# Three added waits in a transformer block whose instruction order is written out by hand

## The chip, the core and the metric

The kernel runs on one NeuronCore of one Trainium2 chip. Five engines work from instruction streams of their own: PE (matrix multiply; PEld is its weight load), DVE (vector), ACT (scalar functions), POOL (general, also elementwise) and SP, which here only issues DMAs. They meet through semaphores alone. The metric is the device time of one execution in microseconds (us); lower is better. Three runs of the kernel before took 273.07, 271.93 and 273.23 us, the median is 273.07.

## The reference

One block of a network on a sequence of 2048 tokens of 448 channels: a modulated layer norm, attention in a sliding window of 256 keys with 16 heads of 28 channels, a gated residual, a second modulated layer norm, a gated MLP whose gate mixes along the sequence with a 2048 x 2048 matrix, and a second gated residual.

```python
mod = silu(c) @ w_mod                      # sa, ca, ga, sb, cb, gb: six rows of 448
h = layernorm(x) * (1 + ca) + sa
q, k, v = split(h @ wqkv)                  # 16 heads of 28
p = softmax(where(0 <= i - j < 256, q @ k.T * 28 ** -0.5, -1e9))
x = x + ga * ((p @ v) @ wo)
h = layernorm(x) * (1 + cb) + sb
z = gelu(h @ w_in)                         # 2 * 896 columns
g = w_sp @ layernorm(z[:, 896:]) + b_sp[:, None]
out = x + gb * ((z[:, :896] * g) @ w_out)
```

## The kernel before

The tokens are 16 tiles of 128, taken in four blocks of four tiles. A tile of `x` is normalised with tokens on partitions (`xn`), turned so that channels lie on partitions (`hT`), modulated, and multiplied by the padded weights of q and k (`WQK`) and of v (`wv`). For the first two blocks PE does the turning (lines 679 and 701), for the later two and for the attention output a DMA transpose does. Scores are exponentiated by ACT into `PA`, masked by DVE, and multiplied by v on PE. After that come the output product with `wo_g` (line 1007), the second norm, the MLP's input products, the mixing along the sequence with `wspA` and `wspB` (line 1133), and the output product (line 1152).

Nothing is scheduled while the kernel runs. Python code first makes a list of operations, each numbered in the order in which it was added, each with a list of the operations that it depends on. The table `ORDER` then says, word by word, which operation goes next on which engine (`p` is PE, `a` ACT, `v` DVE, `g` POOL, `s` SP), and which buffer it takes. `Sched.order` walks the table. `Sched.waits` finds for each operation the semaphore waits that its dependences need, leaving out those that an earlier wait on the same engine already covers, and `emit` writes them ahead of its instruction. A wait holds everything that stands behind it on its engine, since each engine works in order.

The operations that this document follows are these.

- `pad` (lines 590 to 595) copies one 128-row slice of the q or the k weights from `wq_st` into the padded layout of `WQK`, 32 columns a head. There are four slices of each. The last two of k, operations 138 and 139, are copied by POOL at line 595, one behind the other. Then POOL builds the attention mask.
- `stats` and `norm` (lines 597 to 632): DVE takes mean and variance of a tile, POOL raises the variance to the power -1/2 (line 611), DVE forms mean times that (line 615), and DVE or ACT or POOL writes the normalised tile. Operation 163 is the normalised fourth tile of the first block, on DVE at line 623. PE's second set of eight turns (line 679) waits for it.
- The first block's products with `WQK` are at line 726, with the slices of the weights taken one after the other.
- In the third block the four channel slices of `hT` are modulated in place, two by POOL, one by ACT (line 669), one by DVE (line 671, operation 292). PE's line 764 needs all four.
- The gate is folded into `wo`: four POOL products (lines 586 and 587), which stand in the order 129, 130, 128, 131 behind POOL's two slices of `hT`.
- `load2` (lines 400 to 406) splits a load in two, since 448 rows are three times 128 and 64. Operation 20 is the second piece of the load of `w_o`, 64 rows, issued by SP at line 405. On SP it stands between DMA transposes of `w_sp` (line 481).
- Operation 376 is the first group of score matmuls with 64 queries, 64 instructions at line 876.

```python
t_wog = [pool(1.05, lambda e, kc=kc: e.tensor_tensor(wo_g[:, kc, :], wo_g[:, kc, :], gg_sb[:, 0, :], ALU.mult),
              [t_wo, t_gg[0]], -13.0 + 0.1 * kc) for kc in range(DC)]
```

Of the kernel before, what the change touches and what calls it, by code (L numbers as in the profile page):

```python
# [19 lines left out]
2.a 30.v 40.g 41.g 42.g 0.s 31.v 32.v 33.v 43.g 44.g 3.a 4.s 38.g 34.v 5.s 35.v 36.v 37.v 45.g 6.s 59.p.0 60.p.0 52.p.0 54.a 53.a 7.s 51.a 61.p.1 46.g  # L20
146.v 8.s 62.p.1 63.p.0 147.v 1.s 140.v 64.p.0 148.g 9.s 141.v 149.g 65.p.0 142.v 10.s 66.p.0 143.g 150.v 151.a.0 67.p.0 68.p.0 69.p.0 70.p.0 11.s
39.g 144.v 56.p.0 145.v.1 134.g 14.s 57.p 58.p 12.s 167.p.1 132.a 114.v 164.p.2 113.v 133.v 135.g 73.p.3 168.v 16.s 74.p.0 165.v 75.p.0 169.a 152.v
13.s 176.p.0.3 166.a 177.p.4.5 15.s 153.v 158.v 154.g 178.p 179.p 137.a 155.g 17.s 180.p 159.v 181.p 160.v 136.v 185.p 161.g 156.v 183.p 182.p 189.a
190.p.1.2 187.v 191.p.6.7 138.g 157.a.0 162.v 192.p 193.p 163.v.1 139.g 170.p.3 173.p.5 171.v 194.p 234.v 172.v 230.v 228.v 235.v 55.v 231.v 232.v
229.v 233.v 195.p 184.p 198.p 196.p 197.p 174.a 175.a 199.p 186.a 204.p.3 200.a 208.a 203.a 206.p.0 205.p.5 207.p.3 220.p.1 209.v 188.v 211.v 202.a
201.a 210.a 376.p.0.0 377.a.0 378.a 222.p.0 226.p.6 368.p.0.1 221.v 47.g 48.g 236.g 49.g 50.g 237.g 238.v 240.v.0 239.v.1 241.g.2 223.v 242.v.3 227.v
212.p.0 216.v 246.p.1 243.p.4 247.v 244.v 248.v 369.a.0 370.a 372.p.0.2 373.a 374.a 213.p.0 275.v 217.v 245.v 371.v 273.v 277.v 375.v 274.v 115.p.1
380.p.0.1 381.a.1 116.a 382.a 29.s 840.s 20.s 841.s 18.s 846.s 214.p.0 249.p.3 251.p.4 218.a 250.a 384.p.0.3 215.p.7 253.p.0 255.p.3 385.a 252.a 386.a
388.v 279.v 278.v 379.v 280.v 276.v 219.v 397.p.0.1 263.p.4 271.p.1 281.g 282.g 383.v 256.v 283.v 254.v 326.v 324.v 264.v 272.v 398.a.0 399.a
389.p.0.2 224.p.0 257.p.2 285.g.0 284.g.1 286.g.2 287.g.3 390.a.2 391.a 393.p.0.0 394.a 259.p.1 260.a 395.a 225.v 387.v 258.v 400.v 392.v 261.p.0  # L30
401.p.0.1 262.v 552.p.0 535.p.3 536.p 537.p 538.p 569.p.2 570.p 553.p 554.p 539.v 396.v 402.a.3 403.a 405.p.0.4 571.p 555.p 269.p.2 572.p 540.v.0
409.v 556.v 406.a 270.a 407.a 418.p.0.3 419.a.0 404.v 557.v.1 267.p.2 26.s 118.s 21.s 842.s 117.s 19.s 119.s 289.s 288.s 120.s 291.s 290.s 121.s 124.s
123.s 558.s 586.p.0 265.p.0 408.v 268.v 322.v 266.v 410.p.0.1 587.p 588.p 589.p 295.a 293.g 294.g 292.v 300.p.0 573.v 323.v 574.v.2 590.v 320.v 301.v
411.a.0 420.a 414.p.0.0 412.a 296.p.1 302.p.0 415.a 416.a 129.g 130.g 128.g 131.g 325.v 591.v.1 297.v 327.v 321.v 303.v 421.v 413.v 328.g 329.g 417.v
422.p.0.1 423.a.1 575.s 125.s 541.s 845.s 592.s 298.p.1 306.p.0 426.p.0.0 299.a 424.a 427.a 304.p.1 603.p.0 604.p 605.p 606.p 431.p.0.1 307.a 428.a
542.p.0 310.p.4 432.a.2 433.a 430.v 425.v 330.v 607.v 305.v 608.v.0 543.v 311.v 544.v 331.g.0 332.g.1 333.g.2 334.g.3 439.p.0.2 440.a.0 441.a 620.p.3
308.p.0 621.p 435.p.0.0 436.a 437.a 429.v 545.v 309.v 434.v 622.p 593.p.0 623.p 443.p.0.1 444.a.3 445.a 312.p.3 314.p.4 442.v 624.v 594.v 625.v.1
595.v 438.v 315.v 843.s 336.s 338.s 337.s 609.s 335.s 626.s 447.p.0.3 448.a 313.a 449.a 637.p.4 638.p 559.p.2 639.p 460.p.0.0 461.a.1 462.a 451.v
560.v 446.v 610.p.3 654.p.1 640.p 596.v 450.v 611.v 641.v 341.g 597.g 612.v 642.v.2 561.v 452.p.0.3 655.p 656.p 657.p 576.p.3 339.g 658.v 577.v 562.v
659.v.1 546.g 340.g 342.g 598.g 599.g 453.a.0 454.a 456.p.0.0 318.p.0 627.p.1 457.a 458.a 464.p.0.1 465.a.1 455.v 613.v 563.g 547.g 548.g 628.v 564.g  # L40
565.g 463.v 600.g.0 349.p.3 343.p.1 468.p.0.0 350.a 469.a 466.a 470.a 566.g.1 319.v 578.v 344.v 459.v 671.p.4 672.p 347.p.3 348.v 472.v 481.p.0.3
345.p.2 316.p.4 673.p 674.p 482.a.0 346.a 483.a 473.p.0.1 474.a.2 475.a 351.p.3 467.v 317.v 471.v 688.p.3 689.p 23.s 839.s 25.s 27.s 122.s 643.s 24.s
629.v 675.v 352.v 676.v.0 601.g 614.g 549.g.2 567.g 550.g 660.s 602.s 477.p.0.0 690.p 691.p 355.p.0 478.a 479.a 485.p.0.1 486.a.3 487.a 644.p.3
353.p.4 476.v 579.v 484.v 580.g 581.g 356.v 480.v 645.v 489.p.0.4 490.a 491.a 705.p.0 706.p 707.p 708.p 582.g 583.g.0 615.g 584.g 692.v 630.v 354.v
693.v.1 493.v 494.p.0.0 495.a.0 496.a 363.p.1 661.p.0 502.p.0.1 492.v 709.v 631.g 632.g 616.g 488.v 710.v.2 662.v 633.g 497.v 28.s 551.s 126.s 127.g
844.s 677.s 364.v 722.p.0 723.p 678.p.4 679.v 503.a.0 504.a 498.p.0.4 724.p 725.p 359.p.1 499.a 500.a 506.p.0.0 507.a.1 505.v 726.v 727.v.0 634.g.2
360.v 501.v 663.v 514.v 635.g 585.s 694.s 568.s 22.s 728.s 711.s 357.p.2 361.p.0 358.a 510.p.0.2 511.a 739.p.3 740.p 741.p 742.p 508.a 523.p.0.1
695.p.4 646.v 743.v 744.v.1 729.p.1 362.v 696.v 664.v 647.v 648.v 730.v 524.a.0 512.a 515.p.0.4 365.p.4 712.p.1 516.a.2 815.g 617.g.0 816.g 814.g
649.g 650.g 513.v 509.v 618.v 680.v 713.v 366.a 519.p.0.2 517.a 520.a 525.a 756.p.2 757.p 758.p 759.p 527.p.0.3 521.a 528.a.3 531.a 529.a 532.a 745.s
636.s 619.s 746.p.0 651.g.1 652.g 518.v 817.g 863.p.2 864.p.0 865.p 866.p 681.v 760.v 761.v.0 526.v 530.v 665.g 666.g 667.g 682.g 683.g 534.v 522.v  # L50
668.v.0 533.v 669.g 790.p.2 791.p 773.p.3 792.p 793.p 774.p 775.p 776.p 731.v 747.v 794.v 762.s 367.s 653.s 875.a 867.a 763.p.0 670.s 684.g 685.g.2
686.g 795.v.0 697.v 732.v 698.v 733.v 777.v 699.g 700.g 714.v 813.g 778.v.1 764.v 701.v 715.v 734.g 735.g 702.v.1 748.v 703.v 736.v.0 881.p.1 882.p.0
883.p 884.p 1003.p.2 1004.p.3 1005.p 1006.p 819.a 821.a 820.a 885.a 892.a 737.g 818.g 687.s 796.s 779.s 1008.a 1009.a 1007.a 898.p.1 899.p.0 900.p
901.p 1010.a 910.a 902.a 780.p.0 797.p.1 916.p.0 917.p.1 918.p 919.p 704.s 869.v 765.v 766.v 767.v 876.v 886.v 716.g 717.g 718.g 719.v.2 738.s 720.v
810.g 768.g 887.v 769.v 749.v 750.v 893.v 894.a.0 770.v.1 751.g 752.g 771.v 888.v 753.g.0 781.v 889.v 782.v 721.s 783.v 825.v 822.g 824.a 830.s 772.s
855.s 798.v 784.v 920.a 785.g 823.v 799.v 754.v 755.s 800.v 786.v 787.v.2 788.v 927.a 928.v 801.g 802.g 803.g 804.v.1 877.a.0 951.p.2 952.p.0 805.v
929.a.1 933.p.3 953.p 954.p 955.a 962.a 934.p.1 935.p 936.p 937.a 1035.p.2 1036.p.0 1037.p 1038.p 911.g 912.a.0 945.a 789.s 806.s 853.s 859.s 834.s
833.s 849.s 838.s 851.s 852.s 832.s 831.s 856.s 835.s 836.s 837.s 857.s 858.s 861.s 860.s 850.s 848.s 854.s 847.s 862.s 957.v 878.v 868.v 870.v 956.v
938.v 903.v 904.v 890.g 946.g 828.v 826.a 1027.p.1 1041.a 1042.a 1040.a 1039.a 947.a.0 827.v 829.v 921.v 963.v 922.v 939.v 905.v 906.g 968.p.3 969.p.0
970.p 971.p 972.a 980.a 923.v 895.v 958.v 907.g 959.g 913.g 891.v 924.v 930.v 871.v 872.g 873.g 874.g 973.v 974.v 940.v 908.g 981.g 960.g 961.v 896.g  # L60
964.a.0 986.p.2 987.p.3 988.p 990.a 909.g 811.g 992.v 991.v 993.v 994.v 941.v 995.g 996.v 914.g 942.g 1043.p.0 989.p 997.a 965.g 943.g 944.g 1028.p.2
1029.p 1030.p 1044.p.3 1045.p 1032.a 1031.a 1034.a 948.v 975.v 976.g 998.v 1033.a 1011.p.1 1046.p 999.a.0 982.a.1 983.g 931.g 1050.a 1049.a 1047.a
1048.a 1012.p.2 1013.p 1014.p 1015.a 1016.a 1018.a 1017.a 1019.p.3 1051.p.0 1052.p.1 1053.p 1054.p 1020.p.2 1021.p 1022.p 1055.a 1056.a 1058.a 1025.a
1024.a 1057.a 1023.a 1026.a 1000.v 915.v 984.g 977.g 949.g 925.g 879.g 978.v 897.v 985.v 966.g 926.v 950.v 1001.g 932.v 880.v 1002.v 979.g 967.v
1062.p.0 1063.v.0 1065.p.1 1066.v.1 1067.g 1068.p.0 1104.p.1 1105.v.1 1064.g 1106.g 1161.p.2 1173.p.1 1170.p.3 1176.p.4 1174.v.0 1162.v.1 807.g 1175.g
# [1171 lines left out]
```

## Time and profile before

| | us |
|---|---|
| median of three runs (lowest, highest) | 273.07 (271.93, 273.23) |
| the profiled execution | 273.21 |
| its span, first to last instruction | 271.5 |
| PE busy in the span | 262.0 (96%) |
| DVE busy | 160.2 (59%) |
| ACT busy | 132.2 (49%) |
| POOL busy | 124.9 (46%) |

PE is busy nearly throughout, and DVE and ACT are nearly full in the first 110 us, where attention runs; after that PE is alone. The share of an average says little about a single wait. What the change touches lies in the first 48 us, and is read from the timelines of the engines and from the chain of work that ended last, which goes back from the last instruction to what released it at each step. The granted clock of PE is full throughout.

### The profile page before, as it was taken

The numbers are of one execution on the slowest core, as the hardware profiler recorded it, in microseconds if no ns is written. First come the engines' busy times: TensorE is split into PE (matmuls) and PEld (weight loads), VectorE is DVE, ScalarE is ACT, GpSimd is POOL, SyncE is SP. The second block draws the span as 40 slices with busy tenths as digits, with TensorE's granted clock in tenths as the row PEclk, the third lists the DMA queues.
The fourth block names the chain that finished last, engine by engine and source line by source line (L and its number), as shares of the span: only waits on it lengthen the run. The fifth ranks groups of instructions, "written<-read, shape, count | busy, mean of one in ns | idle before, by whom it ended". The sixth has DMA issues, their size and how long they took to land.

```text
span 271.5 us, 6856 instructions
## 1 busy us (share of the span) xinstructions
PE 262.0 (96%) x2918; PEld 135.5 (50%) x2918; DVE 160.2 (59%) x357; ACT 132.2 (49%) x189; POOL 124.9 (46%) x184
## 2 busy tenths in 40 slices
PE   7898999999999999999999999999999999999995
PEld 3654455556476656444444444444444444444453
DVE  6898999999999999885746111123212102251233
ACT  3598999999999994799988300000000000000000
POOL 8530619325949668762499033445313100464130
PEclk9999999999999999999999999999999999999999
DMA  7998532857943567875999970000000000100203
GB/s 224 304 277 171 141 84 46 111 86 117 187 95 80 87 70 161 99 157 106 167 181 195 173 151 0 0 4 0 17 0 2 0 0 0 53 17 0 68 19 101
DMA packets 66777, 25.46 MB, mean 94 GB/s; under 512 B 57845, under 2 KB 66042, under 8 KB 66746
## 3 DMA queue, kind: packets, MB, share of 16 engines
q1 hardware_dynamic: 66472, 24.56, 47.1%
q8 instruction: 23, 0.38, 0.6%
q10 hardware_dynamic: 274, 0.46, 0.5%
q14 instruction: 8, 0.07, 0.1%
HBM read 9.53 MB, written 1.84 MB: 42 GB/s over the span
## 4 chain that ended last, share of the span: by engine, by line
PE 65%; DVE 21%; POOL 5%; ACT 5%; DMA 2%; issue 1%; DVEq 0%; POOLq 0%
PE ps L1133 36%; PE ps L1152 8%; PE ps L1109 7%; PE ps L1063 6%; DVE PA L919 4%; DVE PA L955 3%; DVE st_all L603 3%; PE ps L764 2%; ACT PA L909 2%; POOL rs_all L611 2%; DMA hT<-xn 2%; DVE Vaug L806 2%; PE ps L876 1%; PE ps L1007 1%; DVE o_sb L999 1%
## 5 line engine op out<-in xcount | busy, mean ns | idle before, releaser
L1140 POOL TENSOR_TENSOR z1T<-tmpg,z1T 128x512 bf16<-128x512 bf16 x28 | 31.8, 1154 | 76.2 <-DVE tmpg L1137 76.2
L909 ACT ACTIVATE PA<-ps 128x1536 bf16<-128x1536 f32 (+4 forms) x64 | 60.4, 974 | 2.7 <-PE ps L876 1.7
L1137 DVE TENSOR_TENSOR tmpg<-ps,bsp_bc 128x512 bf16<-128x512 f32 x28 | 19.0, 689 | 62.4 <-PE ps L1133 58.2
L1133 PE MATMUL ps<-wspB,z 128*128 128x512 bf16 x224 | 49.3, 379 | 0.0
L1133 PE MATMUL ps<-wspA,z 128*128 128x512 bf16 x224 | 49.2, 379 | 0.0
L1133 PEld LDWEIGHTS ps<-wspA,z 128*128 128x128 bf16 x224 | 21.8, 98 | 26.5 <-issue 0.4
L1133 PEld LDWEIGHTS ps<-wspB,z 128*128 128x128 bf16 x224 | 21.9, 98 | 26.3
L1163 DVE TENSOR_TENSOR fin<-ps,x_sb 128x448 bf16<-128x448 f32 (+2 forms) x18 | 10.0, 569 | 28.7 <-PE ps L1152 28.7
L611 POOL TENSOR_TENSOR rs_all<-ve_all,neghalf 128x1 f32<-128x1 f32 (+1 forms) x31 | 22.6, 732 | 5.2 <-DVE ve_all L608 3.3
L984 PEld LDWEIGHTS ps<-Vaug,PA 128*128 128x128 bf16 x720 | 20.4, 96 | 5.3 <-issue 1.3
L984 PE MATMUL ps<-Vaug,PA 128*128 128x32 bf16 x720 | 22.2, 176 | 0.4 <-DVE x_sb L1012 0.2
L1063 PE MATMUL ps<-w_in,hT 64*128 64x448 bf16 x224 | 22.3, 349 | 0.2 <-ACT z L1074 0.2
L1152 PE MATMUL ps<-w_out_g,z1T 128*128 128x448 bf16 (+2 forms) x126 | 22.2, 332 | 0.0
L1109 PE MATMUL ps<-hT,w_in 64*128 64x512 bf16 x196 | 21.8, 376 | 0.0
L919 DVE TENSOR_TENSOR PA<-PA,mask 128x1024 bf16<-128x1024 bf16 (+1 forms) x32 | 21.7, 683 | 0.0
L764 PE MATMUL ps<-hT,WQK 128*128 128x512 bf16 x80 | 19.6, 380 | 0.5 <-DVE hT L671 0.5
L603 DVE BATCH_NORM_STATS2 st_all<-x_sb 128x6 f32<-128x448 bf16 x32 | 19.3, 611 | 0.0
L876 PE MATMUL ps<-qT,KT 32*64 32x64 bf16 (+3 forms) x768 | 17.9, 223 | 0.9 <-ACT PA L909 0.3
L608 POOL TENSOR_SCALAR ve_all<-mv_all 128x1 f32<-128x1 f32 (+1 forms) x19 | 6.5, 344 | 25.2 <-DVE mv_all L606 21.0
L940 ACT ACTIVATE PA<-ps 128x1536 bf16<-128x1536 f32 (+1 forms) x16 | 16.4, 1027 | 1.7 <-PE ps L876 1.5
L955 DVE TENSOR_TENSOR PA<-PA,mask 128x2048 bf16<-128x2048 bf16 x14 | 17.0, 1215 | 0.0
L1152 PEld LDWEIGHTS ps<-w_out_g,z1T 128*128 128x128 bf16 x126 | 11.7, 98 | 10.1 <-POOL z1T L1140 0.2
(115 smaller groups left out, 334.7 us busy)
## 6 DMA issues: line engine op xcount, KB each, us to landing
w_in<-in_B_w_in_dram SPq DMA_DIRECT2D x8, 224.0 KB, 4.1
out_dram<-fin SPq DMA_DIRECT2D x15, 112.0 KB, 1.7
x_sb<-in_A_x_dram SPq DMA_DIRECT2D x3, 448.0 KB, 5.3
wmod<-in_w_mod_dram SPq DMA_DIRECT2D x1, 1344.0 KB, 9.7
w_out_g<-in_B_w_out_dram SPq DMA_DIRECT2D x1, 784.0 KB, 5.1
bsp_bc<-in_B_b_sp_dram SPq DMA_DIRECT2D x1, 512.0 KB, 4.3
x_sb<-in_A_x_dram SPq DMA_DIRECT2D x2, 224.0 KB, 3.4
wmod<-in_w_mod_dram SPq DMA_DIRECT2D x2, 224.0 KB, 5.3
```

The costliest lines, as they stand in the source:

```text
L603: st = [dve(0.62 if True else 0, lambda e, t=t, ci=ci, s=s: e.bn_stats(st_all[:, slot, t, ci, :], s()), deps(t), prio) for ci, s in enumer ...
L611: rs = pool(0.41 + 0.155 * len(tiles), lambda e: e.tensor_tensor(rs_all[:, slot, a:b], ve_all[:, slot, a:b], neghalf[:, 0:b - a], ALU.pow) ...
L764: m = pe(4 * MMS, [lambda e, h=h, g=g, kc=kc, tb=tb: e.matmul(ps[:, h.slot[0], :], lhsT=WQK[:, kc, 4 * g:4 * g + 4, :].rearrange("p a b -> ...
L909: return e.activation(cols(place(kb, hf) + 64 + 768 * a, [[384, 2 * (b - a)], [1, w]]), ps[:, h.slot[0]:h.slot[0] + b - a, 2 * n * w:(2 * ...
L919: main_mk[(kb, hf)] = dve(0.15 + 512 * tri / 1920.0, lambda e, hf=hf, tri=tri: e.tensor_tensor(cols(place(kb, hf) + 64, [[384, 8], [192, t ...
L955: return e.tensor_tensor(cols(a, [[d, 2], [384, 16], [1, 64]]), cols(src(), [[0, 2], [64, 16], [1, 64]]), mask_ap([[64 if m else 192, 2], ...
L984: fns.append(lambda e, hO=hO, hd=hd, bi=bi, kb=kb, nb=nb, j=j, c=(2 * t + k) * 384 + 128 * (j - kb), half=half: e.matmul(ps[:, hO.slot[0], ...
L1063: return lambda e, kc, p0, start, stop: e.matmul(ps[:, hs[t % 2].slot[hf], 0:D], lhsT=hT[p0:p0 + 64, kc, t * 128:(t + 1) * 128], rhs=w_in[ ...
L1109: return lambda e, kc, p0, start, stop: e.matmul(ps[:, hs[b // 2].slot[b % 2], :], lhsT=w_in[p0:p0 + 64, kc, ft * 128:(ft + 1) * 128], rhs ...
L1133: m = pe(16 * MMS, [lambda e, h=h, si=si, ft=ft, tb=tb: e.matmul(ps[:, h.slot[0], :], lhsT=z2[:, si, ft * 128:(ft + 1) * 128], rhs=(wspA i ...
L1140: u = pool(1.16, lambda e, ht=ht, ft=ft, tb=tb: e.tensor_tensor(z1T[tb][:, ft, :], tmpg[:, ht.slot[0], :], z1T[tb][:, ft, :], ALU.mult), [ ...
L1152: return [lambda e, ft=ft: e.matmul(ps[:, h.slot[0], c0:c1], lhsT=z1T[t // 4][:, ft, (t % 4) * 128:(t % 4 + 1) * 128], rhs=w_out_g[:, ft, ...
```

## The change

The table `ORDER` is written as one line, and its words are interleaved in another way. The order within each engine, and the buffer of every operation, are the same as before. What differs is a second table, `AFTER`. Each of its pairs adds the first operation to the dependences of the second.

```diff
 ORDER = """
-2.a 30.v 40.g 41.g 42.g 0.s 31.v 32.v 33.v 43.g 44.g 3.a 4.s 38.g 34.v 5.s 35.v 36.v 37.v 45.g 6.s 59.p.0 60.p.0 52.p.0 54.a 53.a 7.s 51.a 61.p.1 46.g
...
 """
+
+AFTER = "376-20 163-138 292-130"
...
         self.prog = {e: [] for e in ENGS}
+        for pair in AFTER.split():
+            first, then = pair.split("-")
+            self.ops[int(then)].deps.add(self.ops[int(first)])
         for word in ORDER.split():
```

Line numbers of the changed kernel are lower by 48 from the loop over `ORDER` on. Its waits differ from those before in three places. The words in brackets name the semaphores that a row waits for: an engine's own, or that of a load.

The first place is POOL at about 10 us: the last two copies of k's weights, with the normalisation of tile three ahead of them and the building of the mask behind. Before:

```order
L608 TENSOR_SCALAR ve_all<-mv_all 128x1 [waits dve]
L611 TENSOR_TENSOR rs_all<-ve_all,neghalf 128x1 [waits pool]
L611 TENSOR_TENSOR rs_all<-ve_all,neghalf 128x1 [waits dve]
L595 COPY WQK<-wq_st 128x16x28 [waits d_wkb]
L595 COPY WQK<-wq_st 128x16x28 [waits d_wkc]
L510 MEMSET mask_60 128x320
```

And changed:

```order
L560 TENSOR_SCALAR ve_all<-mv_all 128x1 [waits dve]
L563 TENSOR_TENSOR rs_all<-ve_all,neghalf 128x1 [waits pool]
L563 TENSOR_TENSOR rs_all<-ve_all,neghalf 128x1 [waits dve]
L547 COPY WQK<-wq_st 128x16x28 [waits d_wkb,dve]
L547 COPY WQK<-wq_st 128x16x28 [waits d_wkc]
L462 MEMSET mask_60 128x320
```

The first of the two copies now waits for DVE as well, for operation 163, the normalised fourth tile; the second copy and the mask stand behind it.

The second place is POOL at about 43 us, where the four products that fold the gate into `w_o` stand behind two slices of `hT`. Before:

```order
L671 TENSOR_SCALAR hT<-hT,modT 128x512 [waits d_h1T2]
L671 TENSOR_SCALAR hT<-hT,modT 128x512
L587 TENSOR_TENSOR wo_g<-wo_g,gg_sb 128x448 [waits d_wob,d_woc,d_woa,d_gg0]
L587 TENSOR_TENSOR wo_g<-wo_g,gg_sb 128x448 x3
L608 TENSOR_SCALAR ve_all<-mv_all 128x4 [waits dve]
```

And changed:

```order
L623 TENSOR_SCALAR hT<-hT,modT 128x512 [waits d_h1T2]
L623 TENSOR_SCALAR hT<-hT,modT 128x512
L539 TENSOR_TENSOR wo_g<-wo_g,gg_sb 128x448 [waits d_wob,d_woc,d_woa,d_gg0]
L539 TENSOR_TENSOR wo_g<-wo_g,gg_sb 128x448 [waits dve]
L539 TENSOR_TENSOR wo_g<-wo_g,gg_sb 128x448 x2
L560 TENSOR_SCALAR ve_all<-mv_all 128x4 [waits dve]
```

The first product is issued as before; the second waits for DVE's slice of `hT` (operation 292), and the last two follow it.

The third place is SP at about 16 us, with two more transposes, a load of `x` and a load of `w_in` queued behind the second piece of `w_o`. Before:

```order
L481 DMA_TRANSPOSE wspA<-in_B_w_sp_dram 128x1024
L405 DMA wo_g<-in_A_wo_dram 64x448
L481 DMA_TRANSPOSE wspA<-in_B_w_sp_dram 128x1024
L409 DMA x_sb<-in_A_x_dram 128x4x448
L481 DMA_TRANSPOSE wspA<-in_B_w_sp_dram 128x1024
L445 DMA w_in<-in_B_w_in_dram 128x896
L577 DMA mod_rows<-gg_sb 1x448 [waits act]
```

And changed:

```order
L433 DMA_TRANSPOSE wspA<-in_B_w_sp_dram 128x1024
L357 DMA wo_g<-in_A_wo_dram 64x448 [waits pe]
L433 DMA_TRANSPOSE wspA<-in_B_w_sp_dram 128x1024
L361 DMA x_sb<-in_A_x_dram 128x4x448
L433 DMA_TRANSPOSE wspA<-in_B_w_sp_dram 128x1024
L397 DMA w_in<-in_B_w_in_dram 128x896
L529 DMA mod_rows<-gg_sb 1x448 [waits act]
```

The load now waits for PE, for operation 376, the first group of 64-query scores, and everything behind it on SP waits with it.

More of the change, by code (lines that the diff above doesn't have):

```diff
@@ L24 @@
[L24 to L63, printed above, removed]
@@ L64 @@
-1024.a 1057.a 1023.a 1026.a 1000.v 915.v 984.g 977.g 949.g 925.g 879.g 978.v 897.v 985.v 966.g 926.v 950.v 1001.g 932.v 880.v 1002.v 979.g 967.v
-1062.p.0 1063.v.0 1065.p.1 1066.v.1 1067.g 1068.p.0 1104.p.1 1105.v.1 1064.g 1106.g 1161.p.2 1173.p.1 1170.p.3 1176.p.4 1174.v.0 1162.v.1 807.g 1175.g
-1163.g 812.g 1177.v.0 1178.g 1069.v.1 1070.g 809.g 1158.p.1 1171.v.0 1164.p.0 1165.v.1 1166.g 1172.g 1167.p.2 1074.p.0 808.g 1159.v.1 1160.g 1168.v.0
-1169.g 1179.p.1 1180.p 1181.v.0 1183.p.2 1187.p.1 1075.v.0 1076.g 1184.p 1188.p 1189.v.1 1098.p.0 1077.p.1 1099.v.0 1100.g 1059.p.0 1060.v.0 1078.v.1
@@ L68 @@
-1079.g 1061.g 1071.p.3 1072.v.1 1185.v.2 1073.g 1092.p.0 1083.p.1 1080.p.2 1089.p.3 1143.p.4 1086.p.5 1110.p.6 1131.p.7 1087.v.3 1182.s 1132.v.0
-1081.v.0 1111.v.1 1112.g 1133.g 1125.p.5 1101.p.2 1126.v.1 1102.v.0 1103.g 1107.p.5 1127.g 1093.v.0 1082.s 1190.s 1088.s 1094.g 1095.p.0 1137.p.2
-1090.v.0 1144.v.1 1145.g 1084.v.1 1108.v.1 1096.v.0 1097.g 1109.g 1116.p.0 1117.v.3 1138.v.0 1139.g 1128.p.1 1113.p.0 1134.p.2 1085.s 1114.v.1 1115.s
-1129.v.0 1186.s 1118.s 1135.v.1 1136.g 1130.g 1091.s 1140.p.0 1141.v.0 1142.g 1119.p.1 1122.p.0 1149.p.2 1155.p.3 1152.p.4 1146.p.5 1191.p.6 1123.v.0
```

6 lines of the change are left out of this document (1 added, 5 removed).

## The prediction

> **What bounds the kernel now.** I read the page first, then the chain that ended last, then the timelines of the engines around the three places.
>
> ```profile
> span 271.5 us, 6856 instructions
> PE 262.0 (96%) x2918; PEld 135.5 (50%) x2918; DVE 160.2 (59%) x357; ACT 132.2 (49%) x189; POOL 124.9 (46%) x184
> q8 instruction: 23, 0.38, 0.6%
> ```
>
> PE is nearly full, so only time in which PE stands idle can be won. The chain (start, length, what), cut to the stretches that the change touches:
>
> ```profile
> 11.46 0.90 DVE xn L623
> 12.40 0.41 PE ps L679 x4
> ...
> 17.19 0.79 PE ps L876 x64
> ...
> 20.54 0.84 PE ps L701 x15
> 21.38 1.09 issue
> 22.47 0.24 PE ps L701
> 22.74 1.00 DVE hT L715 x2
> ...
> 44.08 1.13 DVE hT L671
> ```
>
> The operations that the added waits favour, DVE's L623 and L671, both lie on the chain, and between them is a hole of 1.09 us in which PE waits for nothing that the profile shows. From 45 us on the chain passes between engines that wait for each other, and no load from memory stands in it, so I take what is won at 45 us to reach the end.
>
> **The copies of w_k.** POOL, DVE and PE around 11 us, with uncontended repeats of the two DVE forms at 10.33 and 19.65:
>
> ```profile
> 10.86 1.06 POOL L595 COPY WQK<-wq_st 128x448 bf16<-128x448 bf16 x2
> 16.25 0.23 POOL L608 TENSOR_SCALAR ve_all<-mv_all 128x4 f32<-128x4 f32 x1 [3.67 <-DVE mv_all L606]
> ...
> 7.84 0.73 DVE L688 TENSOR_SCALAR hT<-ps,modT 128x256 bf16<-128x256 bf16 x2
> 10.33 0.15 DVE L615 SCALAR_TENSOR_TENSOR ve_all<-mv_all,rs_all 128x1 f32<-128x1 f32 x1
> 11.00 0.42 DVE L615 SCALAR_TENSOR_TENSOR ve_all<-mv_all,rs_all 128x1 f32<-128x1 f32 x1
> 11.46 0.89 DVE L623 TENSOR_SCALAR xn<-x_sb,mv_all,rs_all 128x448 bf16<-128x448 bf16 x1
> 19.65 0.38 DVE L623 TENSOR_SCALAR xn<-x_sb,mv_all,rs_all 128x448 bf16<-128x448 bf16 x1
> ...
> 12.40 0.62 PE L679 MATMUL ps<-ident,xn 128*128 128x128 bf16 x8 [0.80 <-DVE xn L623]
> 14.28 1.92 PE L726 MATMUL ps<-hT,WQK 128*128 128x256 bf16 x16 [0.27 <-ACT hT L686]
> ```
>
> While POOL copies (10.86 to 11.92), L615 takes 0.42 for 0.15 us and L623 takes 0.89 for 0.38; L623 ends where the copies end plus its own 0.38. With the copies behind it DVE gains 0.27 + 0.51 = 0.78, and L623 ends at 11.57 in place of 12.35. PE was idle for 0.80 before its turns, so these start at about 11.63, 0.77 earlier.
>
> The copies then run from about 11.63 to 12.69, 0.77 later. PE's turns end near 12.1 and its next products want the first copy, ready at 12.2: about 0.1 us, which the 0.27 idle before 14.28 takes up. The mask behind them on POOL is covered by the 3.67 us for which POOL then waits. DVE's next operation beside the copies is L688, whose two at 7.84 took 0.73 together although POOL copied then too, so I charge it nothing. Thus PE comes 0.77 us earlier to L701, whose first fifteen end at 20.6 in place of 21.4.
>
> Whether that is worth anything the hole decides, and this is the term I choose rather than read:
>
> ```profile
> 22.47 0.23 PE L701 MATMUL ps<-ident,xn 128*128 128x128 bf16 x1 [1.09 <-issue]
> ...
> 22.74 1.00 DVE L715 TENSOR_SCALAR hT<-ps,modT 128x512 bf16<-128x512 bf16 x2 [1.17 <-PE ps L701]
> ...
> 10.58 5.57 SPq L481 DMA_TRANSPOSE wspA<-in_B_w_sp_dram  x1
> ...
> q1 hardware_dynamic: 1973, 2.16, 112.1%
> ...
> q8 instruction: 1, 0.02, 33.6%
> q14 instruction: 1, 0.01, 10.4%
> ```
>
> Queue q8 moved 0.38 MB in 23 pieces, some 16 KB each, and PE's 5836 instructions over 23 are about 254 a piece, so I read q8 as PE's instructions. The q1 row is the queues' answer for 12.0 to 19.8 us: the load queue alone, no instructions. The q8 and q14 rows are that for 19.8 to 20.0: one piece on each instruction queue, within 0.2 us of each other, after nothing for 7.8 us. Two streams released together point at the rings, which were working off what SP had issued (the transpose at 10.58 held SP for 5.57 us), not at PE's own pace. None of that moves. So I take the piece to arrive at the same time, PE to resume at 22.47, and the hole to grow from 1.09 to about 1.86. This edit is then worth 0. Its bounds are 0 and 1.86: the hole could move along (0.77 won) or close (0.77 + 1.09). Below 0 it falls only if instructions come later than now, which the fourth rival prices. I take 0 because of the two rows on q8 and q14.
>
> [...]
>
> **The products of w_o.**
>
> ```profile
> 43.00 4.09 POOL L587 TENSOR_TENSOR wo_g<-wo_g,gg_sb 128x448 bf16<-128x448 bf16 x4
> 48.70 0.23 POOL L608 TENSOR_SCALAR ve_all<-mv_all 128x4 f32<-128x4 f32 x1 [1.60 <-DVE mv_all L606]
> ...
> 43.99 1.20 DVE L671 TENSOR_SCALAR hT<-hT,modT 128x512 bf16<-128x512 bf16 x1
> 119.78 0.40 DVE L1032 TENSOR_SCALAR hT<-hT,modT 128x512 bf16<-128x512 bf16 x1
> ...
> 45.25 1.04 PE L764 MATMUL ps<-hT,WQK 128*128 128x512 bf16 x4 [0.51 <-DVE hT L671]
> 53.37 0.93 PE L1007 MATMUL ps<-wo_g,hT 128*128 128x448 bf16 x4
> ```
>
> Four products in 4.09 us are 1.02 each. The first ends at about 44.02, just after L671 is issued; the second then runs beside L671, which takes 1.20 us, while the same form at 119.78, without POOL, takes 0.40. Held back, the second leaves L671 to end at about 44.4 in place of 45.2: 0.80 won on DVE. PE has other work until 45.25 - 0.51 = 44.74, so PE wins 0.51; the rest is lost. The three held products start at about 44.5 and end at 47.6, 0.5 later: POOL then waits 1.60 us anyway, and PE first reads `wo_g` at 53.37. The half microsecond of POOL work that is new to the time after 47.1 falls on DVE work that I charge nothing, since the copy-like DVE operations at 45 to 47 ran beside these same products before.
>
> **The load.** The group it waits for ends at 17.98, so it goes out at 18.0 in place of 16.20, at most 1.8 us later.
>
> ```profile
> 16.20 0.57 SPq L405 DMA_DIRECT2D wo_g<-in_A_wo_dram  x1
> 16.82 2.63 SPq L481 DMA_TRANSPOSE wspA<-in_B_w_sp_dram  x1
> 19.50 0.58 SPq L409 DMA_DIRECT2D x_sb<-in_A_x_dram  x1
> ...
> SPq L577 <- ACT gg_sb L571: 4.0, 1, 4.0
> ```
>
> Behind it SP issues two transposes, a load of x and one of w_in, and then waits 4.0 us for ACT: 1.8 fits in. The piece itself is wanted at 43.00. The load of x would leave at 21.3 (19.50 + 1.8) at the latest; with its form's 5.3 us to landing it is there near 26.6, and DVE takes its first statistics at 31.85:
>
> ```profile
> 31.85 1.14 DVE L603 BATCH_NORM_STATS2 st_all<-x_sb 128x6 f32<-128x448 bf16 x2
> ...
> x_sb<-in_A_x_dram SPq DMA_DIRECT2D x3, 448.0 KB, 5.3
> ```
>
> Worth 0 directly; what the later transposes do to the instruction queue is the last rival.
>
> **The sum.** 0 + 0.51 + 0 off the profiled execution's 273.21 gives 272.7. The median is 0.14 below that execution, which puts the forecast at 272.5 for a median, 0.2% faster. I call within 0.5% (1.4 us) the same, since that is about what a measurement of this kernel tells from no change: its own three runs lie 0.5% apart.
>
> **The rivals.**
> First, the hole is PE's own and moves along: 0.77 + 0.51 = 1.28, so 271.8 as a median. For it: the profile names no fetch. Against: the two instruction queues' common arrival. 0.14.
> Second, the hole closes, because PE asks for its block 0.77 us earlier and that puts it ahead of the transposes in the rings: 0.77 + 1.09 + 0.51 = 2.37, so 270.7. For it: DVE's idle 1.17 before 22.74 leaves room. [...] 0.14.
> Third, the wait at 43 us does nothing, since L671 meets the first product in its place. They overlap by 0.03 us; if POOL came 0.5 us later against DVE it would be so. Then 273.1. 0.10.
> Fourth, slower: the postponed transposes now stand ahead of PE's next block. In 22.4 to 30.3 us PE runs 251 instructions, so the block after is wanted near 30.3; its piece is in the queues' answer for 24.4 to 24.8.
>
> ```profile
> 22.40:30.30 7.90, 7.61 (x125) 3.70 (x126) 7.56 (x19) 7.19 (x10) 0.81 (x2) 1.00 0.66 178
> ...
> q8 instruction: 1, 0.02, 20.3%
> ```
>
> The first piece came at 19.9 and PE went on at 22.47, 2.6 later; by that the next is there at 27.2, 3.1 before it is wanted. A lateness of 1.8 is hidden; beyond 3.1 each us costs one, and above about 5 us the 0.51 is eaten and 0.5% lost. Two holes like the present one more would give 273.1 - 0.5 + 2.2 = 274.8. 0.09.
>
> **The numbers.** The forecast itself has 0.53. Faster by over 0.5% means below 271.7: all of the second rival, and not quite half of the first, which ends at that bound, 0.20. Slower: the fourth and a remainder, 0.10. The same: 0.70. The range takes in the forecast, the first and the third rival and reaches toward the second: 270.9 to 273.7.
>
> **What would show it.** L623 of the first block near 0.38 us and L671 near 0.40 show the two stalls gone; L671's reader on PE without idle time before it shows the 0.51 taken. The idle time before the last L701 tells the cases apart: 1.9 is the forecast, 1.1 the first rival, none the second. SP's wait for ACT should shrink from 4.0 but stay. The forecast is wrong if the hole vanishes, if a new hole named issue stands near 30 us, or if PE waits for POOL's copies at 12 us.

## The result and the profile after

The changed kernel takes 270.92 us (median of 22 runs, 270.06 to 272.09). The kernel before, run beside it on the same chip, takes 272.43 us (22 runs, 270.89 to 273.99). The ratio is 0.9945, with a 95% interval of 0.9929 to 0.9960: 1.5 us are won, between 1.1 and 1.9. The profiled execution took 271.37 us with a span of 269.6, so it is one of the longer ones of the changed kernel; before it was 273.21 and 271.5. In the tables and runs below a few executions took 1 to 2 per cent longer at a lower granted clock (276.18 us at 0.993, 274.92 at 0.994): the medians count them, the ratios do not.

The page of the changed kernel, its span, the engines' busy time and PE's instruction queue (all line numbers are 48 lower than before):

```profile
span 269.6 us, 6840 instructions
PE 261.0 (97%) x2901; PEld 135.7 (50%) x2918; DVE 157.8 (59%) x357; ACT 131.7 (49%) x189; POOL 122.9 (46%) x184
q8 instruction: 23, 0.38, 0.6%
```

PE has 2901 records for the 2918 matmuls of before: 17 are missing from this trace, and one of them matters below. DVE is busy for 2.4 us less, though it does the same work.

The timelines of DVE, POOL and PE around 12 us, and PE's further on to 22 us (start, length, engine, line, operation, count, idle time before):

```profile
11.86 0.15 DVE L567 SCALAR_TENSOR_TENSOR ve_all<-mv_all,rs_all 128x1 f32<-128x1 f32 x1
12.04 0.40 DVE L575 TENSOR_SCALAR xn<-x_sb,mv_all,rs_all 128x448 bf16<-128x448 bf16 x1
...
12.50 1.06 POOL L547 COPY WQK<-wq_st 128x448 bf16<-128x448 bf16 x2 [0.75 <-DVE xn L575]
...
16.42 0.23 POOL L560 TENSOR_SCALAR ve_all<-mv_all 128x4 f32<-128x4 f32 x1 [2.18 <-DVE mv_all L558]
...
9.48 2.98 PE L678 MATMUL ps<-hT,WQK 128*128 128x256 bf16 x23
12.58 0.61 PE L631 MATMUL ps<-ident,xn 128*128 128x128 bf16 x8
...
20.41 1.06 PE L653 MATMUL ps<-ident,xn 128*128 128x128 bf16 x16
21.60 0.40 PE L828 MATMUL ps<-qT,KT 32*128 32x256 bf16 x8
```

Three things differ from the rows of before. DVE's two operations are short, 0.15 and 0.40 us in place of 0.42 and 0.89. PE no longer waits ahead of its turns. And the sixteen turns of L653 run through: the hole of 1.09 us before the last one is gone.

The queues' answer for 16.2 to 16.4 us has the instruction piece that was at 19.9 us before:

```profile
q1 hardware_dynamic: 62, 0.07, 96.8%
q8 instruction: 1, 0.02, 33.5%
```

At 43 us, POOL, DVE and PE:

```profile
42.51 1.04 POOL L539 TENSOR_TENSOR wo_g<-wo_g,gg_sb 128x448 bf16<-128x448 bf16 x1
43.78 3.04 POOL L539 TENSOR_TENSOR wo_g<-wo_g,gg_sb 128x448 bf16<-128x448 bf16 x3 [0.23 <-DVE hT L623]
47.21 0.23 POOL L560 TENSOR_SCALAR ve_all<-mv_all 128x4 f32<-128x4 f32 x1 [0.39 <-DVE mv_all L558]
...
42.76 0.94 DVE L623 TENSOR_SCALAR hT<-hT,modT 128x512 bf16<-128x512 bf16 x1
...
42.45 1.06 PE L936 MATMUL ps<-Vaug,PA 128*128 128x32 bf16 x36
43.99 0.81 PE L716 MATMUL ps<-hT,WQK 128*128 128x512 bf16 x3 [0.47 <-DVE mv_all L558]
44.73 0.40 PE L828 MATMUL ps<-qT,KT 32*128 32x256 bf16 x8
```

The wait holds three of the four products back, but the first one now runs beside DVE's slice of `hT`, which takes 0.94 us and not 0.40. One of PE's four products behind it has no record (x3). Before, the row behind the four began 0.97 us after their start; by that they start at 43.76 here, and PE was idle for about 0.25 us (43.76 less 43.51, the end of the row ahead), not for 0.47. It was 0.51.

SP's timeline in the changed kernel:

```profile
11.21 4.06 SPq L433 DMA_TRANSPOSE wspA<-in_B_w_sp_dram  x1
18.12 0.48 SPq L357 DMA_DIRECT2D wo_g<-in_A_wo_dram  x1
18.64 1.30 SPq L433 DMA_TRANSPOSE wspA<-in_B_w_sp_dram  x1
19.99 0.58 SPq L361 DMA_DIRECT2D x_sb<-in_A_x_dram  x1
20.62 1.22 SPq L433 DMA_TRANSPOSE wspA<-in_B_w_sp_dram  x1
```

And from its waits (total, times, longest):

```profile
SPq L529 <- ACT gg_sb L523: 3.5, 1, 3.5
```

The held load goes out 1.9 us later than before, the two transposes behind it hold SP for 1.30 and 1.22 us, where the first of them held it for 2.63 before, and SP still waits 3.5 us for ACT afterwards. Nothing is late.

### The profile page after: what moved, and what is told of

It is laid out like the page before. It is cut to its first block, busy times and chain, and to the rows that moved or that the text cites. A ratio compares the mean times of both kernels' runs of the same rounds, so it can differ in the third digit from the quotient of the medians.

```text
span 269.6 us, 6840 instructions
## 1 busy us (share of the span) xinstructions
PE 261.0 (97%) x2901; PEld 135.7 (50%) x2918; DVE 157.8 (59%) x357; ACT 131.7 (49%) x189; POOL 122.9 (46%) x184
## 4 chain that ended last, share of the span: by engine, by line
PE 71%; DVE 11%; ACT 9%; POOL 4%; DMA 2%; issue 1%; DVEq 0%; POOLq 0%
PE ps L1085 36%; PE ps L1104 8%; PE ps L1061 7%; PE ps L1015 6%; ACT PA L861 5%; PE ps L716 4%; PE ps L828 3%; DVE st_all L555 2%; PE ps L959 2%; POOL rs_all L563 2%; PE ps L511 2%; ACT PA L892 2%; DMA hT<-xn 2%; PE ps L936 2%; DVE PA L871 2%
## 5 line engine op out<-in xcount | busy, mean ns | idle before, releaser
L1085 PE MATMUL ps<-wspA,z 128*128 128x512 bf16 x219 | 48.6, 379 | 0.4 <-issue 0.2
L563 POOL TENSOR_TENSOR rs_all<-ve_all,neghalf 128x1 f32<-128x1 f32 (+1 forms) x31 | 21.1, 683 | 5.4 <-DVE ve_all L560 3.5
L871 DVE TENSOR_TENSOR PA<-PA,mask 128x1024 bf16<-128x1024 bf16 (+1 forms) x32 | 20.6, 650 | 0.0
L555 DVE BATCH_NORM_STATS2 st_all<-x_sb 128x6 f32<-128x448 bf16 x32 | 19.3, 611 | 0.0
L716 PE MATMUL ps<-hT,WQK 128*128 128x512 bf16 x73 | 18.1, 379 | 1.1 <-DVE mv_all L558 0.5
L892 ACT ACTIVATE PA<-ps 128x1536 bf16<-128x1536 f32 (+1 forms) x16 | 16.4, 1028 | 1.5 <-PE ps L828 1.3
```

The costliest lines, as they stand in the source:

```text
L555: st = [dve(0.62 if True else 0, lambda e, t=t, ci=ci, s=s: e.bn_stats(st_all[:, slot, t, ci, :], s()), deps(t), prio) for ci, s in enumer ...
L563: rs = pool(0.41 + 0.155 * len(tiles), lambda e: e.tensor_tensor(rs_all[:, slot, a:b], ve_all[:, slot, a:b], neghalf[:, 0:b - a], ALU.pow) ...
L716: m = pe(4 * MMS, [lambda e, h=h, g=g, kc=kc, tb=tb: e.matmul(ps[:, h.slot[0], :], lhsT=WQK[:, kc, 4 * g:4 * g + 4, :].rearrange("p a b -> ...
L871: main_mk[(kb, hf)] = dve(0.15 + 512 * tri / 1920.0, lambda e, hf=hf, tri=tri: e.tensor_tensor(cols(place(kb, hf) + 64, [[384, 8], [192, t ...
L1085: m = pe(16 * MMS, [lambda e, h=h, si=si, ft=ft, tb=tb: e.matmul(ps[:, h.slot[0], :], lhsT=z2[:, si, ft * 128:(ft + 1) * 128], rhs=(wspA i ...
```

## Which of the three waits did it

Each wait was tried by itself, and two of them together. The edit is the table alone; the four lines are the copies alone, the products alone, the load alone, and copies and load:

```diff
-AFTER = "376-20 163-138 292-130"
+AFTER = "163-138"
+AFTER = "292-130"
+AFTER = "376-20"
+AFTER = "376-20 163-138"
```

> Only the wait of the copies of w_k is kept. Theory of the prediction (the block of instructions comes when the rings let it through): PE reaches the last turn 0.77 us sooner, the hole before it grows from 1.09 to about 1.9, time as before, within 0.2 us. Rival 1, the earlier request slips ahead of the transposes: the hole closes by this wait alone, 1.9 us less than before. Rival 2, the hole is closed by SP's wait: here it stays, time as before. Rival 3, the hole moves with PE: 1.1 us of hole, 0.8 us less.

> Only the wait of the products of w_o is kept. All theories on the hole: it stays at 1.1 us. Prediction: DVE's slice of hT falls from 1.20 to 0.40 us, PE's idle time of 0.51 before the third block's products goes, 0.5 us less than before. Rival: DVE's slice meets the first product instead, takes 0.9 us, and nothing is won: within 0.2 us of before.

> Only the wait of the load of w_o's second piece is kept. Theory of the prediction: worth nothing, the hole stays, within 0.2 us of before. Rival 1 (the earlier request of PE closes the hole): the same, nothing. Rival 2, SP's silence between 16.2 and 18 us lets PE's block through: the hole closes, 1.1 us less than before, and the first piece on q8 starts near 16.5 us instead of 19.9.

> The waits of the copies and of the load, not that of the products. Theory of the prediction: nothing, since the hole takes up what PE gains. Rival 1 and rival 2 alike: the hole closed and PE 0.77 us sooner, 1.9 us less than before, rival 1 then with the same time as the copies alone, rival 2 with 0.8 us less than the load alone. Rival 3, the hole moves along: 0.8 us less.

Measured beside a kernel before of 271.87 us (35 runs):

| | us, median | ratio to before | 95% interval |
|---|---|---|---|
| copies alone | 271.04 | 0.9964 | 0.9943 to 0.9984 |
| products alone | 271.55 | 0.9989 | 0.9969 to 1.0009 |
| load alone | 271.63 | 0.9993 | 0.9976 to 1.0011 |
| copies and load | 271.17 | 0.9968 | 0.9951 to 0.9985 |

The copies' wait is worth about 1.0 us; the load, at 0.2, adds nothing that can be told from zero, and the products perhaps 0.3. The three by themselves add up to the 1.5 us of the changed kernel, each with half a microsecond of doubt. So the edit that I had costed at nothing carries most of the gain. In the profiles of both kernels that have it the instruction piece starts at 16.2 and 16.5 us and there is no hole; in the two that lack it the piece starts at 19.7 and 19.3 us. That looks like the second rival, the piece that overtakes the transposes. But the two profiles without it have no hole either, though most of what was expected of them kept it: there PE started later and needed the piece later. In the first profile PE went on 2.57 us after the piece's start (19.90 to 22.47); with the products alone the piece starts at 19.66, and the sixteen turns take 1.15 us in place of 1.06, so that kernel just escapes the hole. Two rows of PE with the copies alone, whose 23 products with `WQK` start at 9.48 us as in the changed kernel:

```profile
12.59 0.61 PE L631 MATMUL ps<-ident,xn 128*128 128x128 bf16 x8
...
20.57 1.06 PE L653 MATMUL ps<-ident,xn 128*128 128x128 bf16 x16
```

PE does not wait ahead of its turns here either. Whether the 1.0 us is the hole or DVE's stall was open.

## The piece by itself: moved sooner without the wait, and the load's order turned

First, none of the waits, but the piece sooner. Nine of PE's early warm-up products, which compute nothing that is used, are written as four narrow ones each, so that 27 more products stand ahead of the turns. With some 254 instructions a piece, the prediction's estimate, PE then comes to the end of a piece earlier in its work:

```diff
-AFTER = "376-20 163-138 292-130"
+AFTER = ""
...
-    warm(14, [], 0.44, 1)
+    def warm_narrow(n):
+        for _ in range(n):
+            hW = Hold(bA)
+            hW.until.append(pe(0.44, [lambda e, hW=hW, k=k: e.matmul(
+                ps[:, hW.slot[0], 128 * k:128 * k + 128], lhsT=ident[:], rhs=ident[:],
+                start=True, stop=True) for k in range(4)], [t_ident], 900.0, [hW]))
+
+    warm_narrow(9)
+    warm(5, [], 0.44, 1)
```

> None of the three waits. Nine of PE's early warm-up products are written as four narrow ones each (128 columns in place of 512, the same columns in all), so that 27 more instructions stand ahead of PE's turns and the end of PE's first instruction piece is passed before PE waits for the fourth normalised tile. Theory 'order in the rings' (what the copies' wait won is that PE asks for its next piece sooner, within about 2.2 us of the issue of the first transposed load): the piece starts at 14 to 16.5 us, ahead of the transposed load's 256-byte packets, no idle time named issue stands near 22 us, although L615's and L623's counterparts still take 0.42 and 0.89 us; the time falls by 0.3 to 1.1 us against before, to 270.9 to 271.6. Rival 'DVE's stall' (what was won is DVE's 0.78 us, and the piece's place costs nothing outside the one profile): the time stays that of before, within 0.3 us.

It took 272.18 us; before, beside it, 272.25 (ratio 1.0001, 0.9982 to 1.0019). The timelines of its DVE and PE (line numbers 8 above the changed kernel's):

```profile
11.34 0.42 DVE L575 SCALAR_TENSOR_TENSOR ve_all<-mv_all,rs_all 128x1 f32<-128x1 f32 x1
11.80 0.89 DVE L583 TENSOR_SCALAR xn<-x_sb,mv_all,rs_all 128x448 bf16<-128x448 bf16 x1
...
8.96 2.98 PE L686 MATMUL ps<-hT,WQK 128*128 128x256 bf16 x23 [0.27 <-DVE hT L648]
12.74 0.62 PE L639 MATMUL ps<-ident,xn 128*128 128x128 bf16 x8 [0.80 <-DVE xn L583]
...
20.59 1.06 PE L661 MATMUL ps<-ident,xn 128*128 128x128 bf16 x16
```

Its instruction queue in 11.8 to 12.0 us:

```profile
q8 instruction: 1, 0.02, 41.7%
```

The piece is there 8 us sooner than in the first profile of before, no hole stands at 22 us, DVE's stall is untouched, and the time is that of before. So in a typical execution the late piece costs nothing that the runs show; the interval leaves room for 0.5 us either way. What the narrow products cost by themselves was not measured apart, but PE's turns and the sixteen turns come as late behind the 23 products as before (3.78 and 11.63 us).

Second, the changed kernel with the first transposed load one place sooner on SP, which was to push the piece behind it again:

```diff
 ORDER (SP's words; 840 is the transpose, 29 the load of w_o)
-17.s 29.s 840.s 20.s
+17.s 840.s 29.s 20.s
```

> The changed kernel with one exchange on SP: the first transposed load goes ahead of the first load of w_o instead of behind it, so it is issued 0.56 us sooner. Theory 'order in the rings': PE passes the end of its piece 2.6 us after that issue in place of 2.03, and the piece waits behind the transposed load again: it starts near 19 to 19.9 us, an idle time named issue of 0.8 to 1.9 us is back before the last of the turns L653 near 22 us, and the time is that without the copies' wait, 0.5 to 1.1 us above the changed kernel. Rival 'DVE's stall': DVE's two operations are at 0.15 and 0.40 us as in the changed kernel, so the time is that of the changed kernel within 0.3 us.

It took 270.85 us (ratio 0.9948, 0.9931 to 0.9965), as the changed kernel. The transpose went out at 10.16 us, in place of 11.21, yet the piece started at 16.0 us as in the changed kernel. So the theory of a fixed distance between PE's request and that issue fell; this kernel could not bring the hole back. Its PE and DVE at 43 us are of use for the products:

```profile
42.50 0.41 DVE L623 TENSOR_SCALAR hT<-hT,modT 128x512 bf16<-128x512 bf16 x1
...
9.22 2.98 PE L678 MATMUL ps<-hT,WQK 128*128 128x256 bf16 x23 [0.29 <-DVE hT L640]
...
43.10 1.02 PE L716 MATMUL ps<-hT,WQK 128*128 128x512 bf16 x4
44.05 0.40 PE L828 MATMUL ps<-qT,KT 32*128 32x256 bf16 x8
```

DVE's slice met the gap between POOL's first product and the held ones: 0.41 us, and PE does not wait. What the wait at 43 us takes thus differs between two executions of one POOL order.

## All four products behind DVE's slice

The wait is put on the first of POOL's products, not the second:

```diff
-AFTER = "376-20 163-138 292-130"
+AFTER = "376-20 163-138 292-129"
```

> The changed kernel with the wait put on the first of POOL's four products of w_o instead of the second, so that none of the four runs before the turned tile hT is done. If the first product is what still doubles L623's counterpart of 0.94 us in the changed kernel: it takes 0.40 us, the 0.47 us for which PE stood idle behind it go, and the time falls by 0.2 to 0.5 us against the changed kernel, to about 270.5. If instead POOL's four products become late for their reader (PE's product with wo_g at 51.9 us; they would end near 47.7 us) or DVE meets them elsewhere: no change or slower.

270.86 us, ratio 0.9944 (0.9924 to 0.9964). Its POOL, DVE and PE:

```profile
42.39 4.03 POOL L539 TENSOR_TENSOR wo_g<-wo_g,gg_sb 128x448 bf16<-128x448 bf16 x4 [1.45 <-DVE hT L623]
...
41.91 0.40 DVE L623 TENSOR_SCALAR hT<-hT,modT 128x512 bf16<-128x512 bf16 x1
...
8.62 2.98 PE L678 MATMUL ps<-hT,WQK 128*128 128x256 bf16 x23
...
42.50 1.02 PE L716 MATMUL ps<-hT,WQK 128*128 128x512 bf16 x4
43.46 0.40 PE L828 MATMUL ps<-qT,KT 32*128 32x256 bf16 x8
```

The slice takes 0.40 us and PE's idle time is gone, as expected; POOL's later work is not late. In the time it cannot be told from the changed kernel, so this version is no proven improvement.

## Does every execution of before have the hole?

My prediction took the hole from one profile. The program of before was profiled two more times:

```diff
-AFTER = "376-20 163-138 292-130"
+AFTER = ""
```

> None of the three waits, that is the program of before once more, for a second profile of it. Theory 'floor' (without the copies' wait the piece lands at a time of its own, and PE goes on at 21.9 to 22.5 us whenever it started; an execution that starts late reaches that point late anyway and shows no hole): instruction piece at 19.2 to 19.9 us, PE's last turn L653 at 21.9 to 22.5 us, idle time before it between 0 and 1.3 us, the smaller the later the first loads were issued. If every execution of before has the full hole: idle of 1.1 us again.

> The program of before a third time, for one more profile of it. If the hole of 1.09 us belongs to rare executions, as the second profile says: none here or under 0.5 us, PE's second stop at 21.3 to 22.2 us, and a time near 272. If the second profile was the exception: idle time named issue of about 1 us before the last turn, and a time near 273.

They took 272.07 and 271.96 us, spans 270.4 and 270.2. The timeline of PE in the first of them:

```profile
8.90 2.98 PE L678 MATMUL ps<-hT,WQK 128*128 128x256 bf16 x23
12.64 0.62 PE L631 MATMUL ps<-ident,xn 128*128 128x128 bf16 x8 [0.76 <-DVE xn L575]
...
20.51 1.06 PE L653 MATMUL ps<-ident,xn 128*128 128x128 bf16 x16
...
45.08 0.40 PE L828 MATMUL ps<-qT,KT 32*128 32x256 bf16 x8
```

Its instruction queue in 18.2 to 18.3 us:

```profile
q8 instruction: 1, 0.02, 73.5%
```

No hole: the sixteen turns run through, and the piece started at 18.2 us in both, early enough for them (18.2 and the 2.57 us of the first profile make 20.8). The expected 19.2 to 19.9 us for the piece were missed. Of three profiled executions of the same program one has the hole, and that one took 273.21 us where the other two took about 272.

## The wait with the piece late, and with the piece sooner

To part the two causes from the other side, PE was also made to come to the end of a piece later in its work, by leaving out eight of the early warm-up products, without the waits and with the copies' wait; and the copies' wait was put on top of the narrow products. The first two kernels, with either line of the table:

```diff
 ORDER (PE's words)
-62.p.1 63.p.0 64.p.0 65.p.0 66.p.0 67.p.0 68.p.0 69.p.0
...
-AFTER = "376-20 163-138 292-130"
+AFTER = ""
+AFTER = "163-138"
```

The third is the kernel with the narrow products, and one line:

```diff
-AFTER = ""
+AFTER = "163-138"
```

> None of the three waits, and eight of PE's early warm-up products left out (they compute nothing that is used), so that PE passes the end of its first instruction piece 16 instructions later in the program, near 15 us. It is the control for the next kernel. Floor theory: piece at 19 to 20 us, PE's second stop 16 instructions further on, at about the same 22 us; time that of before, 272.0 to 272.6.

> The copies' wait alone, with the same eight warm-up products left out: DVE's stall is gone, but PE passes the end of its piece about 1 us later than with the wait alone, near 14.2 us, as late as without it. Floor theory: the piece waits behind the transposed load again (19 to 20 us), a hole of 0.5 to 1.5 us is back near 22 us, and the wait is worth 0 to 0.4 us against the kernel without waits and with the same eight left out. If the stall alone counts and the hole belongs to rare executions: 0.8 to 1.0 us below that kernel, 271.1 or so, hole or not.

> The copies' wait alone, with nine warm-up products written as four narrow ones each, so that the piece is asked for before the turns with or without the wait; against the same arrangement without the wait (272.18) it gives the worth of DVE's stall with no hole in either. If the stall is worth its 0.8 us at the end: 271.2 to 271.5, as the copies' wait alone in the usual arrangement. If what was won hung on the piece: 272.2.

Before, beside them, took 272.07 us (29 runs). Without the eight products: 271.84 us with no wait (ratio 0.9990, 0.9967 to 1.0014) and 272.00 with the copies' wait (0.9995, 0.9973 to 1.0016). That looks like what the floor theory expects, since the wait is worth nothing here, but the profiles show another reason. The timelines of PE and DVE with the copies' wait and the eight left out, then PE's row of before:

```profile
9.04 4.54 PE L678 MATMUL ps<-hT,WQK 128*128 128x256 bf16 x23
...
12.27 0.42 DVE L706 CAST qT<-ps 128x256 bf16<-128x256 f32 x1 [1.94 <-PE ps L678]
12.62 0.15 DVE L567 SCALAR_TENSOR_TENSOR ve_all<-mv_all,rs_all 128x1 f32<-128x1 f32 x1
12.80 0.40 DVE L575 TENSOR_SCALAR xn<-x_sb,mv_all,rs_all 128x448 bf16<-128x448 bf16 x1
```

```profile
8.62 2.98 PE L726 MATMUL ps<-hT,WQK 128*128 128x256 bf16 x23
```

PE's 23 products take 4.54 us in place of 2.98, DVE waits 1.94 us for them, and by then, I take it, POOL's copies are over where they did not wait: DVE's two operations are at 0.15 and 0.40 us in the kernel without the wait too. There was no stall left to remove, and the wait is worth nothing: that fits the stall as the cause. On the hole the pair says little. The piece was late in both, at 18.9 us without the wait and 19.8 with it, and the hole that was expected near 22 us is in neither. The two kernels should not have been built on a change of the warm-up.

The copies' wait over the narrow products took 271.21 us (0.9974, 0.9954 to 0.9994). Without the wait the same arrangement stood at 1.0001 of before. With the piece out of the way in both, the wait is worth 0.27% or 0.7 us by these two ratios. That is the size of DVE's stall, with no hole in it, but the two intervals overlap between 0.9982 and 0.9994, so this pair alone does not prove it. The one profile of the kernel is of its longest execution, 276.18 us, and is left out below.

## Where the time went

Executions start up to 1 us apart, so the profiles are compared from one point of PE's work, the start of its 23 products with `WQK` (the x23 rows). Worked out from the rows shown and the same rows of the other profiles:

| profile | fourth tile's turns after | sixteen turns begin after | score products behind `hT` begin after |
|---|---|---|---|
| before, first profile (hole) | 3.78 | 11.76 | 37.60 |
| before, second | 3.74 | 11.61 | 36.18 |
| before, third | 3.74 | 11.58 | 36.16 |
| block sooner, no wait | 3.78 | 11.63 | 36.29 |
| copies alone | 3.11 | 11.09 | 35.66 |
| products alone | 3.74 | 11.59 | 35.58 |
| load alone | 3.74 | 11.59 | 35.85 |
| copies and load | 3.10 | 10.93 | 35.12 |
| changed kernel | 3.10 | 10.93 | 35.25 |
| transpose sooner | 3.10 | 10.93 | 34.83 |
| all products | 3.10 | 10.93 | 34.84 |

Each kernel of the table with the copies' wait is 0.63 to 0.68 us ahead at the turns and 0.5 to 0.7 at the sixteen turns. The first profile of before is 1.4 us behind its own repeats, of which 1.09 is the hole. At 45 us the changed kernel is 0.9 us ahead of the second and third profile of before, and the two kernels whose slice of `hT` took 0.4 us are 1.35 ahead. From there to the end of the span every profile of the table takes 224.6 to 225.3 us (before 271.5 - 46.2, the changed kernel 269.6 - 44.7). So what is won at 45 us arrives at the end, as far as a spread of 0.7 us lets one see.

The way from the second column to the third follows the length of DVE's slice of `hT`, whichever wait shortened it. It is 24.6 to 24.7 us where the slice takes about 1.20 (the repeats of before, copies alone, block sooner), 24.3 where it takes 0.94 (the changed kernel), 24.2 to 24.3 where it takes 0.54, and 23.9 to 24.0 where it takes 0.40 to 0.46. The 0.54 stands in the two profiles with the load's wait and without that of the products, load alone and then copies and load:

```profile
43.79 0.54 DVE L623 TENSOR_SCALAR hT<-hT,modT 128x512 bf16<-128x512 bf16 x1
```

```profile
42.76 0.54 DVE L623 TENSOR_SCALAR hT<-hT,modT 128x512 bf16<-128x512 bf16 x1
```

There POOL begins its four products 2.08 us ahead of the slice, against 0.99 in the first two profiles of before, so the slice meets them at another point. With one profile of each kernel it is not shown that the load's wait brings this about.

The measured 1.5 us of the changed kernel is more than the 0.9 of its profile, which the interval of 1.1 to 1.9 does not reach. Some longer executions belong to the gap: of 103 runs of before in the four comparisons 25 took 272.5 us or more, and of 69 runs of the six kernels that have the copies' wait and keep the warm-up products none did. The hole can be part of that, but not all, since the kernel with the piece sooner and no wait, whose profile has the piece at 11.8 us and no hole, has 4 such runs of 12, and with eight warm-up products left out it is the kernel with the wait that has 2 and the one without that has none. What slows those was not found.

## The prediction, step by step

**What bounds the kernel.** Held: PE's idle time in the first 48 us was what there was to win, and what was won at 45 us reached the end.

**The copies of w_k.** The part up to PE held. L615 and L623 went from 0.42 and 0.89 to 0.15 and 0.40 us (predicted 0.15 and 0.38), PE's turns came 0.68 us sooner (predicted 0.77), POOL's later copies held nobody up, and POOL's next wait, 2.18 us in place of 3.67, covered the mask. Beside POOL's work the same form of DVE is longer in the rows: `xn` takes 0.89 us beside a copy and 0.40 without one, and the slice of `hT` 1.20 (before) and 0.94 (changed kernel) beside a product and 0.40 without one. Why is not shown. How much is added does not follow from POOL's rows: with the products alone the slice starts 0.30 us before the row of POOL's first product ends and takes 0.46.

The step that failed is the next: "So I take the piece to arrive at the same time, PE to resume at 22.47, and the hole to grow from 1.09 to about 1.86. This edit is then worth 0." It is worth about 1.0 us by the runs with the copies alone (0.4 to 1.55), and the profiles show 0.7 of that on PE's path. Two things were wrong in it. The hole was a property of one execution, not of the kernel: two more profiles of the same program lack it, and closing it alone won nothing. And the piece does not come at a fixed time: it started at 19.9, 18.2 and 18.2 us in three executions of before and at 15.8 to 16.5 in the five profiles with the copies' wait and the usual warm-up. The two rows on q8 and q14, on which I rested the choice, do not bear it: in the changed kernel the piece on q8 is at 16.3 us while that on q14 stays at 19.6, so the two are not released together there.

The runs that I had would have warned me. Three runs of before spread over 1.3 us, 271.93 to 273.23, which is about the size of the hole, and the profiled one stood at the upper end. A stall that no row gives a cause for, in one execution, should have been weighed against the fastest run.

**The products of w_o.** The mechanism held and the size was off. 0.51 us was the whole idle time of PE; the changed kernel's profile took about half of it (0.25 left), because the first product met the slice, as the third rival had it for one execution. With the slice clear of POOL the idle time went entirely, in three other profiles. The runs with the products alone give 0.3 us, from a loss of 0.2 to a gain of 0.8.

**The load.** Held by the runs, not by the profiles: 0.2 us with an interval from a loss of 0.3 to a gain of 0.7, where the term was 0. The profiles with this wait stand 0.3 us (load alone) and 0.5 us (copies and load against copies alone) ahead at 45 us, by the shorter slice; a way from the load to DVE's slice was not in the prediction. The rest held: SP's wait for ACT shrank from 4.0 to 3.5 and stayed, and no new hole came near 30 us. The fourth rival did not happen.

**The rivals.** The first gave the right size, 0.77 + 0.51 = 1.28, and 1.35 was found on PE's path where the slice ran clear; but its reason, a hole of PE's own that moves along, was not the true one, for there was mostly no hole. The second rival's picture was seen, the piece ahead of the transposes and no idle time, but its 1.09 us is not there to be won in a typical execution. When PE asks for a piece (the block of the second rival) stands in no trace; the runs show when one starts, at 19.9 us in the first profile of before and at 16.3 in the changed kernel. By the profiles the sum of 0.51 should have been 0.5 to 0.7 for the copies and 0.25 to 0.7 for the slice.

**The number.** The forecast of 272.5 us stands 1.6 above the 270.92. Of that 0.6 is the kernel before, whose median of 273.07 in three runs became 272.43 in 22; the gain was put at 0.5 us and measured at 1.5. The 270.92 lies in the stated range by 0.02 us, which is luck: the range reached that far for the sake of the first two rivals, whose reasons were not the true ones. By the prediction's own mark of 0.5% for "the same", to which it gave 0.70, the changed kernel is faster, by 0.55% (0.40 to 0.71).

**What would show it.** The idle time before the last L701 was to tell the cases apart, "none the second". It read none, and the second rival still was not the cause, since two of the three profiled executions of before read none as well. The mark was good for one profile and not for the kernel.

## What to carry to other kernels

Beside a copy on POOL a short DVE operation on the path took 0.89 us here, and 0.40 without it. Holding the copy back by one wait moved the cost to an engine that had slack (POOL's next wait went from 3.67 to 2.18 us), and the gain reached the end, since PE waited for DVE there, for 0.80 us. An idle stretch without a named releaser that stands in one profile should be looked for in a second execution before a sum is built on it, and its size set beside the spread of the runs. An experiment that moves the end of an instruction piece should leave the warm-up products in: with eight of them left out 23 products took 4.54 us here in place of 2.98.

## What was not expected of the hardware

With fewer warm-up products a later stretch took longer. Without eight of them PE was busy for only 0.49 of the 2 us from 4 to 6 (all 2.00 before), and its 23 products with `WQK` took 4.54 us in place of 2.98, while the granted clock in the profile stayed at 1.00. The answer by stretches, for the kernel with the copies' wait and the eight left out:

```profile
4.00:6.00 2.00, 0.49 (x10) 0.32 (x10) 1.42 (x6) 0.05 (x1) 1.83 (x4) 1.00 1.07 345
8.00:10.00 2.00, 2.00 (x8) 1.01 (x7) 1.90 (x7) 1.57 (x4) 0.94 (x3) 1.00 1.06 289
```

What made the products longer is not shown: the column of the granted clock is at 1.00 in both stretches. The medians of the two kernels are no higher than before's all the same, and where they regain it was not followed.

The other surprise is when an instruction piece starts. In ten profiles with the usual warm-up the first piece on q8 behind the turns started at 15.8 to 16.5 us where the turns began at most 2.7 us after SP issued a load of four tiles of `x` (at 10.12 us in the changed kernel, 2.46 ahead of its turns), and at 18.2 to 19.9 where they began 3.0 us or more after it (at 9.38 and 12.40 in the first profile of before). This was only read off; no run moved that load. The first five of the ten all have the copies' wait and the other five all lack it, so the distance cannot be told from the wait by them alone. One more profile speaks for the distance: with the copies' wait and eight warm-up products left out the turns began 4.15 us after that load, and the piece started at 19.8 us.
